# Retention attention and an MLP on one core: block 6's first product by seven half-size products, q and k turned each on its own landing, later scores, a new order

## The chip, the cores and the metric

The kernel runs on one core of a Trainium2 chip. The metric is device time in microseconds (us), the median of several runs. Beside the timed runs there is one profiled execution with a trace; its span is the time from the first to the last instruction that the profiler recorded.

## The reference

Eight batches of eight heads, 576 positions, 64 values per head. Position i attends to all j up to i with a weight that falls as gamma^(i-j), without softmax. The heads are joined to 512 values per token (4608 tokens), and a two-layer MLP with exact gelu follows.

```python
scores = scale * np.matmul(q, k.transpose(0, 1, 3, 2))
gamma = 1.0 - 2.0 ** (-5.0 - np.arange(H))
Dmat = np.where(rel >= 0, gamma ** rel, 0.0)      # rel = i - j
attn = np.matmul(scores * Dmat, v)
x = attn.transpose(0, 2, 1, 3).reshape(B * S, H * D)    # 4608 x 512
g = gelu(x @ w_in)                                       # 512 x 2048
out = g @ w_out                                          # 2048 x 512
```

## The kernel before, in words

**Units and blocks.** The attention is cut into 36 units, numbered 0 to 35: a unit is 128 positions of one batch (or the last 64 positions of two batches together). From unit 4 on, units are handled in groups of two batches (4 and 5, ..., 33 and 34), with the short ones alone (10, 17, 26, 35). Four units in a row make one block of 512 tokens for the MLP; there are nine blocks, 0 to 8. Unit n belongs to block n // 4.

**A group's way through the attention.** Its q, k and v are loaded and cast to bf16 by DMAs issued on POOL (`load`, L318). q and k are turned so that the head's 64 values lie on the partitions: for the first seven groups by TensorE (`turn`, L478), for all later ones by transposing DMAs issued on SP's queue (`turn_dma`, L489), which also carries most of the stores of the output (L718). Then follow the scores (`scores`, L526, for a short unit L516, into four or two PSUM banks), the mask on VectorE (`masked`, L549 and L545), the product with v (`inner`, L591 or L582), the running state of the recurrence (`state`, L610), the part of the earlier positions (`cross`, L642) and the copy of the result to the tile xT (`evacuate`, L661 or L457). v is scaled beforehand (`scaled_v`, on VectorE L566 or, for units in the set BY_ACT, in eight pieces on ACT, L563).

**The first product of a block** (x @ w_in) is made in the ordinary way for blocks 0 to 6 (`mlp1`, L690): 16 pieces of 128 rows of d_ff, each four matmuls of up to 512 columns, then the gelu on ACT (L699). From block FAST on (7 before) it is made by seven products of half size in place of eight (`fast`, L955, a Strassen scheme in Winograd's form). The products are named P1 to P7; d_ff is cut in four groups j of 512, a group has seven products of four matmuls of 256 columns. They need sums of blocks of w_in (`sum_in`, L913 to L915, and `sum_last`, L920, which overwrites a part of w_in once block FAST - 1 has read it) and sums of blocks of x (`sum_x`, L928). Between the products there are copies of a bank (P1 and P7, L452 on VectorE or L457 on ACT, whichever the planner thinks free), additions on VectorE (P6 L970, P5 L974), and the gelus (L976, L980).

**The second product** (g @ w_out) is made by `mlp2` (L735) for block 0 and in the same seven-product way for blocks 1 to 8 (`part`, L874, with sums of g on VectorE, L771 to L775, and `after` for what follows each product).

**What sets the order.** Every engine works through its own list of instructions in order. The lists are written by a planner that runs while the kernel is built: it keeps a reckoned clock for each engine (`T`), reckoned landings for DMAs (`hw_dma`, `sw_dma`), and a main loop (L1179 on) that appends, at each step, the work that is ready by this reckoning: X (cross), U (state), S (inner and/or scores), T (turn), or a piece of the MLP (`mlp_pick`). `fire` (L1121) lists what other engines do beside it: loads in the order of ORDER, sums, scaled v, and the transposing DMAs. The runs of the MLP are first product, second product, block after block; a second product and the seven-product first product of the next block are mixed piece by piece (kinds "3" and "4"), up to two groups j at a time.

**ORDER** (L330) lists the loads (`q5`, `wi3` a piece of w_in, `wo2` a piece of w_out, `io` constants, `dq3` a decay table), and among them numbers that steer the planner: `a8` puts unit 8's scaled v on ACT; `s20+3.0` lets the scores of the group that begins with unit 20 be listed only 3.0 us after the turn's reckoned landing; `b17+2.0` does the same for the product with v of unit 17. nA counts the units that are scored, nB those multiplied with v, nX those finished, nD the groups whose turn by DMA is listed.

Of the kernel before, what the change touches and what calls it, by code (L numbers as in the profile page):

```python
# [17 lines left out]
def kernel(  # L18
# [14 lines left out]
    nc = tc.nc  # L33
# [13 lines left out]
    NCI = -(-S // C)  # L47
# [4 lines left out]
    units = [(bp, 0, j) for bp in range(2) for j in range(2)]  # L52
# [7 lines left out]
    N_U = len(units)  # L60
# [7 lines left out]

    N_PE_TR = 7
    HW_FIRST = ((("q", 0),), (("k", 0),))  # L70
    FAST, ALL_FAST = 7, 7
    N_LD = 5
    N_QKT = 4
    N_VH = 6
# [250 lines left out]
    for x, keys in enumerate(zip(*HW_FIRST)):  # L325
        for n, (what, i) in enumerate(keys):
            land[what, i] = (4.6, 5.2)[n] + 0.75 * x
            t = tiles_of(i)
            cast_due[what, i] = (t[1] if what == "v" else t[0][:, "qk".index(what)], first[what, i])
    ORDER = ("wi1 q1 k1 wi0 io q2 k2 v0 v1 q3 wi2 v2 wi3 k3 wi4 v3 q4 wi5 wi6 q5 k4 a8 dq2 k5 wo1 wi7 wo0 v5 v4 "  # L330
# [4 lines left out]
             "b22+3.0 s23+2.0 s15+0.3 s13+3.0").split()  # L335

    BY_ACT = {int(x[1:]) for x in ORDER if x[0] == "a"}
    S_LATE = {int(x[1:].split("+")[0]): float(x.split("+")[1]) for x in ORDER if x[0] == "s"}
    B_LATE = {int(x[1:].split("+")[0]): float(x.split("+")[1]) for x in ORDER if x[0] == "b"}
    ORDER = [x for x in ORDER if x[0] not in "abs"]  # L340

    rest = const.tile([128, 2], BF16, name="rest")

# [137 lines left out]
        release(b, done + 0.05)  # L481
        sg[n]["T"] = max(sg[n].get("T", 0.0), done + SEM)

    def turn_dma(n):
        qk, qkT = loaded[groups[n][0]][0], qkT_of(n)
        short = units[groups[n][0]][2] is None
        rows = TAIL if short else C
        for jj in range(2):
            nc.sync.dma_start(qkT[:, jj, :, 0:rows], qk[0:rows, jj].rearrange("p h j d -> p (h j d)"), transpose=True)  # L489
            ends = sg[n].setdefault("ends", {})  # L490

            def put(end, jj=jj):
                ends[jj] = end
                sg[n]["T"] = max(ends.values()) + SEM

            hw_dma(1.3, MOVE["turn"] * (0.62 if short else 1.0), max(land["qk"[jj], i] for i in groups[n]), put)

    def scores(n):
        g = groups[n]
# [121 lines left out]

    def state_at(bp, ci):
        at = u_ready.get((bp, ci - 1), 1e9) if ci else 0.0
        return max([at] + [st[i].get("V", 1e9) if "Bdone" in st[i] else 1e9 for i in pair_of[bp, ci]])

    def reload():
# [372 lines left out]
    def fast_ready(t, j, p):  # L999
        if any((t, n) not in xs_at for n in range(4)) or any((2 * j + x, y) not in wi_at for x in range(2) for y in range(2)):  # L1000
            return 1e9
        at = max([xs_at[t, {P7: 1, P6: 2, P4: 3}.get(p, 0)]] + [wi_at[2 * j + x, y] for x in range(2) for y in range(2)])
        if p == P1:
            if not may_begin(t, j):
                return 1e9
            if wanted[0] and lead()[0] == "3" and lead()[2] in (M3, M4, M1) or len(held) + 3 + pending() > 7:
                return 1e9
            if t >= ALL_FAST and nA < N_U and lead()[0] == "3":
                return 1e9
            if j == 2 and t < ALL_FAST and (t - 1, M1, 0) not in begun:  # L1010
                return 1e9
            return max(at, free_time(2))
        if p == P7:
            return max(at, free_time(1), f_at.get(((t, j - 2), "V"), f_at.get(((t - 1, j + 2), "V"), 0.0) if j < 2 else 1e9))
        at = max(at, f_at[(t, j), {P6: P1, P2: P1, P5: P6, P4: P6, P3: P5}[p]])
        return max(at, free_time(1)) if p == P6 else at
# [104 lines left out]
    def fire():  # L1121
        nonlocal nD, nV
        now = T["pe"]
        while ORDER and T["pool"] <= now + 1.5 and next_order():
            pass
        while T["dve"] <= now + 1.5:
            one = min((x for x in queued if x[0] <= now + 0.2 and may_sum(*x[2:])), key=lambda x: x[1], default=None)
            if one is None:
                break
            queued.remove(one)  # L1130
            one[2](*one[3])
        if FAST < N_BLK and len(wi_sum) < 3 * (N_DF // 2) and first_block() >= 3 and T["dve"] <= now + (0.0 if first_block() < FAST - 1 else 0.8):
            sum_in(len(wi_sum) // 3)
        for mm in list(wi_read):
            if (mm, 0) in wi_at and T["dve"] <= now + 1.0 and wi_at[mm, 0] <= now + 0.3 and wi_read[mm] <= now + 0.3:
                sum_last(mm)
                del wi_read[mm]
        t = xs_next[0]
        if (t < N_BLK and all(4 * t + y in x_at for y in range(4)) and (t == FAST or all((t - 1, j) in f_done for j in range(0, N_DF // 4, 1 + (t - 1 < ALL_FAST))))
                and max(x_at[4 * t + y] for y in range(4)) <= now + 0.3 and T["dve"] <= now + 1.0):  # L1140
            sum_x(t)
            xs_next[0] += 1
        for key in [x for x in cast_due if land[x] <= now + 0.2]:
            dst, src = cast_due.pop(key)
            land[key] = either(0.7, land[key], dst, src) + SEM
        while later:
            n = next((n for n, x in enumerate(later) if x[0] <= now and T[x[1]] <= now + 0.25
                      and (x[1] == "dve" or x[0] < 5.0 or all(y[3] is not make_args for y in later))), None)
            if n is None:
                break  # L1150
            _, engine, dur, fn = later.pop(n)
            fn()
            on(engine, dur, now)
        while nV < N_U and nV < len(s_done) + N_VH and ("v", v_order[nV]) in land and ("v", v_order[nV]) not in cast_due:
            i = v_order[nV]
            if land["v", i] + 0.1 > now or nA <= i or i in kept and nA < 8 or i in raw and (T["act"] if i in BY_ACT else T["dve"]) > now + 2.0 * (nA > 8):
                break
            scaled_v(i)
            nV += 1
        while (nD < len(groups) and nD < group_of[min(nX, N_U - 1)] + N_QKT  # L1160
               and all((what, i) in land and land[what, i] - 0.3 <= now for what in "qk" for i in groups[nD])):
            turn_dma(nD)
            nD += 1
            store_kept()

    def warm(n):
# [12 lines left out]
    while True:  # L1179
# [21 lines left out]
        if nA < N_U:  # L1201
            n = group_of[nA]
            if n < nT or N_PE_TR <= n < nD:
                g, scored = groups[n], sg[n]["T"] + S_LATE.get(nA, 0.0)
        back = list(range(nB, nA))
        if nB < nA:
            if early:
                back = [nB]
            first_o = units[nB][1] == 0 and units[nB][2] == 0
            ready = max(max(st[i]["R"], land["v", i] if i in raw and nA < 8 else st[i].get("V", 1e9)) for i in back)  # L1210
            if any(("v", i) in cast_due for i in back):
                ready = 1e9
            ready = max(ready + B_LATE.get(back[0], 0.0), free_time(out_banks(back) + first_o))
            hurry = early or nA == N_U or stuck
            if not hurry and first:
                kind, t = first[0], first[1]
                hurry = nB < 4 * t + 4 if kind in "14" else len(runs[0]) <= (20 if t + 1 >= FAST else 6) and nB < 4 * t + 8
            if hurry:
                n = out_banks(back) + first_o + 2 * len(g)
                along = not early and nA >= 4 and scored <= now and len(frees(n)) == n and free_time(n) <= now + 0.3  # L1220
                cand(ready, "S", g if along else [], back)
        if g and scored < 1e8:
            if early or stuck:
                cand(max(scored, free_time(2 * len(g))) if nA - nB <= 2 else 1e9, "S", g, [])
            else:
# [4 lines left out]
                if (free and all(st[i]["R"] <= now and st[i].get("V", 1e9) <= now + 0.3 for i in back)  # L1230
                        and nA + len(g) <= ahead):
                    n = 2 * len(g) + out_banks(back) + any(units[i][1] == 0 for i in back)
                    wanted[0] = scored <= now and nA < 4 * (first[1] - (first[0] == "4")) + 12
                    if n + len(held) + pending() <= 8 and T["dve"] <= now + 1.0:
                        cand(max(scored, free_time(n) - 0.3), "S", g, back)
                    elif n > 7 and n - 2 * len(g) + len(held) + pending() <= 8:
                        cand(free_time(n - 2 * len(g)) - 0.3, "S", [], back)
# [52 lines left out]
        soon = [x for x in (land[key] for key in cast_due)] + [x[0] for x in queued] + [T["dve"] for x in queued]  # L1290
        if nV < N_U and ("v", v_order[nV]) in land and nV < len(s_done) + N_VH:
            soon += [land["v", v_order[nV]] + 0.1, T["dve"] - 1.9]
        if nD < len(groups) and all((x, i) in land for x in "qk" for i in groups[nD]):
            soon.append(max(land[x, i] for x in "qk" for i in groups[nD]) - 0.3)
        if wanted[0]:
            soon += [T["dve"] - 1.0 + 0.01]
        waits = [w for w in waits + soon if w > now and w < 1e8]
# [37 lines left out]
```

## Time and profile before

| | us |
|---|---|
| median of three timed runs | 287.1 (286.86 to 287.55) |
| profiled execution | 288.85 |
| its span | 287.1 |
| granted TensorE clock | 1.00 |

Costly groups of the page, busy us and instructions: first product L690 101.7 (624 matmuls), second product L874 46.8 + 32.2 + 30.6 (912), seven-product first product of blocks 7 and 8 L955 33.4 in four rows (224); on VectorE the masks L549 30.2 + 10.3, sums of g 21.7 + 21.4 + 13.3; on ACT the gelus L699 66.2. The DMA engines are busy nearly all the time until some 210 us, first with loads; POOL issues the last load at 179.8 us.

How to read it: PE is TensorE's matmuls, PEld its weight loads, DVE is VectorE, ACT ScalarE, POOL GpSimd, SP the queue of SyncE. A group's mean is that of an instruction from its start to its end; matmuls overlap, so the spacing of a stream is read from the chain (length divided by count). The chain of waits is the work that ended last, followed back.

### The profile page before, as it was taken

The numbers are of one execution on the slowest core, as the hardware profiler recorded it, in microseconds if no ns is written. First come the engines' busy times: TensorE is split into PE (matmuls) and PEld (weight loads), VectorE is DVE, ScalarE is ACT, GpSimd is POOL, SyncE is SP. The second block draws the span as 40 slices with busy tenths as digits, with TensorE's granted clock in tenths as the row PEclk, the third lists the DMA queues.
The fourth block names the chain that finished last, engine by engine and source line by source line (L and its number), as shares of the span: only waits on it lengthen the run. The fifth ranks groups of instructions, "written<-read, shape, count | busy, mean of one in ns | idle before, by whom it ended". The sixth has DMA issues, their size and how long they took to land.

```text
span 287.1 us, 7914 instructions
## 1 busy us (share of the span) xinstructions
PE 278.1 (97%) x3310; PEld 202.3 (70%) x3310; DVE 192.1 (67%) x400; ACT 153.2 (53%) x346; POOL 114.0 (40%) x143
## 2 busy tenths in 40 slices
PE   7989999999999999899999999999999999999994
PEld 2568677578864688348855686468755888888893
DVE  4834682789865795788098817673589659966922
ACT  4956436664549524773258438872566363565320
POOL 8997888995245355325667434100000000000000
PEclk9999999999999999999999999999999999999999
DMA  9999999999999999999999999990220000400234
GB/s 144 169 178 184 187 182 156 142 124 128 159 153 249 157 134 127 156 196 147 167 177 165 147 135 138 219 103 1 75 75 0 2 0 2 146 2 1 75 110 112
DMA packets 152803, 35.38 MB, mean 123 GB/s; under 512 B 141120, under 2 KB 148928, under 8 KB 152768
## 3 DMA queue, kind: packets, MB, share of 16 engines
q0 software_dynamic: 116832, 18.10, 93.7%
q1 hardware_dynamic: 34528, 16.26, 34.8%
q10 hardware_dynamic: 1408, 0.52, 0.7%
q8 instruction: 26, 0.43, 0.6%
q14 instruction: 9, 0.07, 0.1%
HBM read 36.70 MB, written 9.44 MB: 161 GB/s over the span
## 4 chain that ended last, share of the span: by engine, by line
PE 76%; DMA 16%; POOL 4%; DVE 2%; issue 1%; POOLq 0%; SPq 0%
PE m L874 28%; PE hT L690 26%; PE f L955 9%; DMA qk_ld<-in_q_dram 5%; PE oT L735 5%; DMA qk_ld<-in_k_dram 4%; DMA qkT<-qk_ld 4%; DMA qk<-in_k_dram 3%; PE o_ps L591 2%; PE sc L526 2%; POOL qk L318 2%; PE qk_ps L478 1%; POOL w_in L291 1%; PE u_ps L610 1%; PE o_ps L642 1%; POOL v_ld L318 1%
## 5 line engine op out<-in xcount | busy, mean ns | idle before, releaser
L690 PE MATMUL hT<-xT,w_in 128*128 128x512 bf16 (+3 forms) x624 | 101.7, 319 | 0.0
L699 ACT ACTIVATE g<-hT 128x512 bf16<-128x512 f32 (+2 forms) x121 | 66.2, 564 | 41.6 <-PE hT L690 41.1
L690 PEld LDWEIGHTS <-w_in 128*128 128x128 bf16 x624 | 54.7, 98 | 39.9
L874 PEld LDWEIGHTS <-gs 128*128 128x128 bf16 x656 | 62.3, 98 | 7.6
L874 PE MATMUL m<-w_sum,gs 128*128 128x256 bf16 (+1 forms) x400 | 46.8, 268 | 0.1
L318 POOL DMA_DIRECT2D v_ld<-in_v_dram x40 | 34.1, 860 | 22.3 <-DMA qk_ld<-in_k_dram 11.3
L549 DVE TENSOR_TENSOR ret<-sc,msk 128x512 bf16<-128x512 f32 x48 | 30.2, 682 | 15.2 <-PE sc L526 15.0
L318 POOL DMA_DIRECT2D qk_ld<-in_k_dram x36 | 30.3, 850 | 23.1 <-DMA qk_ld<-in_q_dram 21.0
L318 POOL DMA_DIRECT2D qk_ld<-in_q_dram x36 | 30.6, 855 | 19.2 <-DMA qkT<-qk_ld 5.4
L874 PE MATMUL m<-w_out,gs 128*128 128x256 bf16 x256 | 32.2, 273 | 0.0
L874 PE MATMUL m<-w_sum,g 128*128 128x256 bf16 x256 | 30.6, 273 | 0.0
L563 ACT ACTIVATE vh<-v_ld,dv 128x64 bf16<-128x64 bf16 x112 | 27.9, 337 | 0.0
L874 PEld LDWEIGHTS <-g 128*128 128x128 bf16 x256 | 25.1, 98 | 4.0
L771 DVE TENSOR_TENSOR gs<-g 128x1024 bf16<-128x1024 bf16 x32 | 21.7, 686 | 7.6 <-ACT g L699 7.4
L661 DVE TENSOR_TENSOR xT<-o_ps,dqT 128x512 bf16<-128x512 f32 (+1 forms) x32 | 18.4, 616 | 5.4 <-PE o_ps L642 5.1
L775 DVE TENSOR_TENSOR gs<-g 128x1024 bf16<-128x1024 bf16 x32 | 21.4, 682 | 0.0
L457 ACT COPY o<-m 128x512 f32<-128x512 f32 x14 | 8.2, 585 | 22.8 <-PE m L874 22.8
L826 DVE SCALAR_TENSOR_TENSOR o<-m,o 128x512 f32<-128x512 f32 (+1 forms) x9 | 5.6, 629 | 18.7 <-PE m L874 10.1
L980 ACT ACTIVATE g<-f 128x512 bf16<-128x512 f32 x24 | 13.6, 591 | 6.9 <-PE f L955 6.9
L457 ACT CAST u_sb<-u_ps 128x512 bf16<-128x512 f32 x14 | 8.2, 585 | 16.4 <-PE u_ps L610 16.4
L735 PE MATMUL oT<-w_out,g 128*128 128x512 bf16 x64 | 15.5, 380 | 0.0
L549 DVE TENSOR_TENSOR ret<-sc,near 128x512 bf16<-128x512 f32 x16 | 10.3, 683 | 7.2 <-PE sc L526 6.0
(96 smaller groups left out, 303.9 us busy)
## 6 DMA issues: line engine op xcount, KB each, us to landing
out_dram<-o SPq DMA_DIRECT2D x27, 256.0 KB, 7.1
v_ld<-in_v_dram POOLq DMA_DIRECT2D x32, 128.0 KB, 8.9
qk_ld<-in_q_dram POOLq DMA_DIRECT2D x28, 128.0 KB, 9.6
qk_ld<-in_k_dram POOLq DMA_DIRECT2D x28, 128.0 KB, 10.7
w_in<-in_moe_w_in_dram POOLq DMA_DIRECT2D x8, 256.0 KB, 6.8
w_out<-in_moe_w_out_dram POOLq DMA_DIRECT2D x8, 256.0 KB, 8.2
out_dram<-o SPq DMA_DIRECT2D x14, 128.0 KB, 2.3
qk_ld<-in_k_dram POOLq DMA_DIRECT2D x8, 64.0 KB, 9.6
```

The source lines that it names most:

```text
L318: nc.gpsimd.dma_start(dst, src[2 * bp + jj, :, ci * C:ci * C + n, :].rearrange("h s d -> s h d"))
L457: nc.scalar.copy(dst, src)
L549: nc.vector.tensor_tensor(r, t, by, op=ALU.mult)
L563: nc.scalar.activation(vh[:, h, :], loaded[i][1][:, h, :], AF.Copy, scale=dv[:, h, ci:ci + 1])
L661: nc.vector.tensor_tensor(x_of(i)[:, :, n * x:n * x + n], o, dqT[:, :, ci * C:ci * C + n], op=ALU.mult)
L690: nc.tensor.matmul(hT[:, m, :], lhsT=w[:, cc, o:o + 128], rhs=x_tiles[t][:, cc, lo:hi], start=(cc == 0), stop=(cc == N_DM - 1))
L699: nc.scalar.activation(g_of(t, m0 // 2)[:, m0 % 2:m0 % 2 + n, lo:hi], hT, AF.Gelu)
L735: nc.tensor.matmul(oT, lhsT=g_of(t, m // 2)[:, m % 2, cols], rhs=w_out_sb[m // 2][:, m % 2, :], start=(m == 0), stop=(m == N_DF - 1))
L771: nc.vector.tensor_tensor(s.rearrange("p m a b -> p m (a b)"), g[:, :, 0, :], g[:, :, 1, :], op=ALU.add)
L775: nc.vector.tensor_tensor(s, g[:, :, :, LEFT], g[:, :, :, RIGHT], op=MINUS)
L874: nc.tensor.matmul(m[:, 0 if apart else ts, :], lhsT=a, rhs=w[:, c0:c1], start=p in begins and mm == 0 and ts == 0, stop=mm == N_DF // 2 - ...
L955: nc.tensor.matmul(m[:, y, :], lhsT=a[:, c], rhs=d[:, c], start=p in (P1, P7) and y == 0 and c == 0, stop=c == 1, skip_group_check=True)
```

## The change

Seven edits, all in the code that the planner runs.

- FAST and ALL_FAST go from 7 to 6: block 6's first product is made by seven half-size products too, all four groups of it. The sums of w_in are then made once for blocks 6, 7 and 8, and those of x for block 6 as well.
- `turn_dma` lists the transposing DMA of q or of k alone, as soon as that one's loads are reckoned landed (`turnable`); before, both were listed when both had landed.
- Groups that are turned by DMA have their scores listed 2.5 us behind the turn's reckoned landing where ORDER has no number for them (before 0).
- The beginning of a seven-product group: the old rules (not while attention is left, and a rule on the third group) make room for a list, P_WAIT (`p25+35`: group 1 of block 6, number 4 x 6 + 1, not before 35 units are scored).
- Two more numbers per unit or block: DVE_LAG (`z`), how far VectorE's reckoned clock may be ahead when scores are listed (before 1.0 for all), and HURRY (`u`), when waiting units' products are listed ahead of the MLP's pieces.
- `state_at` keeps the second state of a pair of batches behind the last unit of the pair before.
- ORDER is another list.

```diff
@@ -68,7 +68,7 @@
 
     N_PE_TR = 7
     HW_FIRST = ((("q", 0),), (("k", 0),))
-    FAST, ALL_FAST = 7, 7
+    FAST, ALL_FAST = 6, 6
     N_LD = 5
     N_QKT = 4
     N_VH = 6
@@ -327,17 +327,21 @@
             land[what, i] = (4.6, 5.2)[n] + 0.75 * x
             t = tiles_of(i)
             cast_due[what, i] = (t[1] if what == "v" else t[0][:, "qk".index(what)], first[what, i])
-    ORDER = ("wi1 q1 k1 wi0 io q2 k2 v0 v1 q3 wi2 v2 wi3 k3 wi4 v3 q4 wi5 wi6 q5 k4 a8 dq2 k5 wo1 wi7 wo0 v5 v4 "
-             "wo3 wo2 q6 wo6 q8 dq3 wo7 v7 wo4 k6 k7 wo5 q7 v6 v9 v11 k9 q9 k8 k10 s4+0.6 q10 k11 k12 v8 q12 a29 "
-             "v10 dq4 s31+0.6 s27+6.0 a27 a6 a20 q11 v12 a28 a7 s34+4.0 a19 b6+0.3 b21+1.5 b7+2.0 s21+3.0 b10+4.0 "
-             "s8+0.6 s11+0.3 b17+2.0 s32+6.0 b19+6.0 s2+0.3 b23+1.0 b18+1.0 s18+1.0 a13 s16+0.3 a11 s20+3.0 "
-             "s29+6.0 s10+1.5 a14 a25 b2+0.6 b20+4.0 a32 s25+6.0 b15+0.3 b13+3.0 s12+0.6 a33 s14+0.3 s26+0.6 "
-             "b22+3.0 s23+2.0 s15+0.3 s13+3.0").split()
+    ORDER = ("wi1 k1 wi0 io q1 v0 q2 k2 v1 wi2 v2 k3 wi3 q3 v3 wi4 wi5 wi6 k4 q5 k5 q4 v5 wi7 wo1 wo0 k6 v4 dq2 "
+             "wo2 wo3 q7 wo4 k7 dq3 q11 b4+1.0 wo6 v8 wo5 q6 k8 wo7 v6 v7 k9 q10 q9 a28 k11 q8 v11 k10 q12 dq4 v9 "
+             "v10 a5 k12 v12 b19+6.0 a24 a27 a26 s4+1.5 z32+3 z8+5 b11+1.5 a23 z23+2.2 s2+0.6 p32+28 p31+28 z18+5 "
+             "z31+1.6 s21+1.0 s14+1.5 b14+4.0 z19+0.6 z5+0.3 z13+5 s10+4.0 z27+2.2 z34+2.2 b17+1.0 a0 b3+1.0 "
+             "p25+35 z30+0.3 p33+26 z28+0.3 z17+2.2 s1+1.0 s31+6.0 z16+0.3 z4+0.3 z22+0.6 s16+3.0 s23+3.0 b22+0.3 "
+             "a14 b16+2.0 b15+2.0 a11 z14+3 p35+31 s27+0.6 z10+5 z20+2.2 s9+4.0 a18 a30 z12+2.2 s22+3.0 s35+0.6 "
+             "s8+1.5 s29+0.6 z15+5 u2+8 b5+0.3 p28+29 s5+6.0 s26+1.5 p26+28 b13+2.0 p29+29 u5+20 s19+4.0 p24+31 a7 "
+             "a20 b9+1.0 s24+0.3 s28+0.6 a17 b18+3.0 a22 u4+28 b12+1.5 s33+1.5 s7+1.5 s30+0.3 u8+0 s32+4.0 z21+0.6 "
+             "b21+6.0").split()
 
     BY_ACT = {int(x[1:]) for x in ORDER if x[0] == "a"}
     S_LATE = {int(x[1:].split("+")[0]): float(x.split("+")[1]) for x in ORDER if x[0] == "s"}
     B_LATE = {int(x[1:].split("+")[0]): float(x.split("+")[1]) for x in ORDER if x[0] == "b"}
-    ORDER = [x for x in ORDER if x[0] not in "abs"]
+    DVE_LAG, P_WAIT, HURRY = ({int(x[1:].split("+")[0]): float(x.split("+")[1]) for x in ORDER if x[0] == kind} for kind in "zpu")
+    ORDER = [x for x in ORDER if x[0] not in "abszpu"]
 
     rest = const.tile([128, 2], BF16, name="rest")
 
@@ -481,19 +485,24 @@
         release(b, done + 0.05)
         sg[n]["T"] = max(sg[n].get("T", 0.0), done + SEM)
 
-    def turn_dma(n):
+    def turn_dma(n, jj):
         qk, qkT = loaded[groups[n][0]][0], qkT_of(n)
         short = units[groups[n][0]][2] is None
         rows = TAIL if short else C
-        for jj in range(2):
-            nc.sync.dma_start(qkT[:, jj, :, 0:rows], qk[0:rows, jj].rearrange("p h j d -> p (h j d)"), transpose=True)
-            ends = sg[n].setdefault("ends", {})
-
-            def put(end, jj=jj):
-                ends[jj] = end
-                sg[n]["T"] = max(ends.values()) + SEM
-
-            hw_dma(1.3, MOVE["turn"] * (0.62 if short else 1.0), max(land["qk"[jj], i] for i in groups[n]), put)
+        nc.sync.dma_start(qkT[:, jj, :, 0:rows], qk[0:rows, jj].rearrange("p h j d -> p (h j d)"), transpose=True)
+        ends = sg[n].setdefault("ends", {})
+
+        def put(end):
+            ends[jj] = end
+            sg[n]["T"] = max(ends.values()) + SEM
+
+        hw_dma(1.3, MOVE["turn"] * (0.62 if short else 1.0), max(land["qk"[jj], i] for i in groups[n]), put)
+
+    def turnable(now):
+        if nD >= len(groups) or nD >= group_of[min(nX, N_U - 1)] + N_QKT:
+            return None
+        return next((jj for jj in range(2) if jj not in sg[nD].get("ends", {})
+                     and all(("qk"[jj], i) in land and land["qk"[jj], i] - 0.3 <= now for i in groups[nD])), None)
 
     def scores(n):
         g = groups[n]
@@ -621,6 +630,8 @@
 
     def state_at(bp, ci):
         at = u_ready.get((bp, ci - 1), 1e9) if ci else 0.0
+        if bp and ci == 1 and nX <= units.index((bp - 1, NCI - 1, None)):
+            return 1e9
         return max([at] + [st[i].get("V", 1e9) if "Bdone" in st[i] else 1e9 for i in pair_of[bp, ci]])
 
     def reload():
@@ -1005,9 +1016,7 @@
                 return 1e9
             if wanted[0] and lead()[0] == "3" and lead()[2] in (M3, M4, M1) or len(held) + 3 + pending() > 7:
                 return 1e9
-            if t >= ALL_FAST and nA < N_U and lead()[0] == "3":
-                return 1e9
-            if j == 2 and t < ALL_FAST and (t - 1, M1, 0) not in begun:
+            if nA < P_WAIT.get(4 * t + j, 0):
                 return 1e9
             return max(at, free_time(2))
         if p == P7:
@@ -1157,10 +1166,12 @@
                 break
             scaled_v(i)
             nV += 1
-        while (nD < len(groups) and nD < group_of[min(nX, N_U - 1)] + N_QKT
-               and all((what, i) in land and land[what, i] - 0.3 <= now for what in "qk" for i in groups[nD])):
-            turn_dma(nD)
-            nD += 1
+        while True:
+            jj = turnable(now)
+            if jj is None:
+                break
+            turn_dma(nD, jj)
+            nD += len(sg[nD]["ends"]) == 2
             store_kept()
 
     def warm(n):
@@ -1201,7 +1212,7 @@
         if nA < N_U:
             n = group_of[nA]
             if n < nT or N_PE_TR <= n < nD:
-                g, scored = groups[n], sg[n]["T"] + S_LATE.get(nA, 0.0)
+                g, scored = groups[n], sg[n]["T"] + S_LATE.get(nA, 2.5 if n >= N_PE_TR else 0.0)
         back = list(range(nB, nA))
         if nB < nA:
             if early:
@@ -1214,7 +1225,7 @@
             hurry = early or nA == N_U or stuck
             if not hurry and first:
                 kind, t = first[0], first[1]
-                hurry = nB < 4 * t + 4 if kind in "14" else len(runs[0]) <= (20 if t + 1 >= FAST else 6) and nB < 4 * t + 8
+                hurry = nB < 4 * t + 4 if kind in "14" else len(runs[0]) <= HURRY.get(t, 8 if t + 1 >= FAST else 16) and nB < 4 * t + 8 + 4 * (t + 1 >= FAST)
             if hurry:
                 n = out_banks(back) + first_o + 2 * len(g)
                 along = not early and nA >= 4 and scored <= now and len(frees(n)) == n and free_time(n) <= now + 0.3
@@ -1231,7 +1242,7 @@
                         and nA + len(g) <= ahead):
                     n = 2 * len(g) + out_banks(back) + any(units[i][1] == 0 for i in back)
                     wanted[0] = scored <= now and nA < 4 * (first[1] - (first[0] == "4")) + 12
-                    if n + len(held) + pending() <= 8 and T["dve"] <= now + 1.0:
+                    if n + len(held) + pending() <= 8 and T["dve"] <= now + DVE_LAG.get(nA, 1.0):
                         cand(max(scored, free_time(n) - 0.3), "S", g, back)
                     elif n > 7 and n - 2 * len(g) + len(held) + pending() <= 8:
                         cand(free_time(n - 2 * len(g)) - 0.3, "S", [], back)
@@ -1290,8 +1301,10 @@
         soon = [x for x in (land[key] for key in cast_due)] + [x[0] for x in queued] + [T["dve"] for x in queued]
         if nV < N_U and ("v", v_order[nV]) in land and nV < len(s_done) + N_VH:
             soon += [land["v", v_order[nV]] + 0.1, T["dve"] - 1.9]
-        if nD < len(groups) and all((x, i) in land for x in "qk" for i in groups[nD]):
-            soon.append(max(land[x, i] for x in "qk" for i in groups[nD]) - 0.3)
+        if nD < len(groups):
+            for x in "qk":
+                if all((x, i) in land for i in groups[nD]):
+                    soon.append(max(land[x, i] for i in groups[nD]) - 0.3)
         if wanted[0]:
             soon += [T["dve"] - 1.0 + 0.01]
         waits = [w for w in waits + soon if w > now and w < 1e8]
```

## The prediction

> **What bounds the kernel now.** I read the busy table first, then PE's waits, then the chain of waits in order of time, then the busy time by stretch. In the first line the reader is to see that TensorE (PE) is busy nearly all the time; the next three are all that PE waited for after its first instruction (waited-for time, times, longest).
>
> ```profile
> PE 278.1 (97%) x3310; PEld 202.3 (70%) x3310; DVE 192.1 (67%) x400; ACT 153.2 (53%) x346; POOL 114.0 (40%) x143
> ```
>
> ```profile
> PE sc L526 <- DMA qkT<-qk_ld: 1.7, 1, 1.7
> PE qk_ps L478 <- DMA qk<-in_k_dram: 1.2, 1, 1.2
> ...
> PE qk_ps L478 <- DVE qk L452: 0.5, 1, 0.5
> ```
>
> So of 287.1 us, PE is idle for 9.0: 1.2 before it starts, the 3.4 of these waits, 0.3 of smaller gaps, and 4.1 at the end, where the last output is stored. The first 19.4 us also hold 30 warm-up matmuls (9.4 us), so work begins to be plentiful there. After that a us of matmuls taken away is a us off the span, unless something new makes PE wait. The chain of waits around block 6 (start, length, what) shows this without a hole, and gives the price of the two kinds of product:
>
> ```profile
> 205.95 6.91 PE hT L690 x32
> 212.85 0.57 PE o_ps L591 x16
> 213.42 0.25 PE u_ps L610 x16
> 213.67 0.30 PE sc L516 x12
> ...
> 214.27 3.56 PE hT L690 x16
> 217.83 0.25 PE o_ps L582 x16
> 218.07 0.13 PE o_ps L642 x16
> 218.20 3.56 PE hT L690 x16
> 221.76 2.18 PE m L874 x20
> 223.94 0.87 PE f L955 x8
> ```
>
> The hT lines are block 6's first product, 64 matmuls of 512 columns; f at L955 is block 7's, already made by seven half-size products. Between them lie the last attention units: unit 35's scores start at 213.67.
>
> **Part 1, block 6's first product.** 6.91 / 32 = 0.216 us for a matmul of 512 columns, 0.873 / 8 = 0.109 for one of 256. Removed: 64 x 0.216 = 13.82 us. Added: four groups of d_ff, seven products each, four matmuls in a product: 112 x 0.1092 = 12.23. PE saves 1.59 us. Nothing hides this: PE is the engine whose end sets the end here, and blocks 7 and 8 show (no PE wait from 221.8 to 283) that such products interleaved with a second product can run without a hole.
>
> The page TensorE: Matmul & The Clock Gate of the Trainium skill (Back-to-back issue gap) speaks against this: in a stream with weight loads it has about 131 ns for a matmul of 512 columns and 81 for one of 128. By a line between these two (an estimate from that page, some 98 ns at 256) the removed work would be 8.4 us, the added 10.9, and the change would cost 2.5. Its other formula there, columns / 2.4 + 2.5 ns, gives 215.8 and 109.2 and so the saving above. This trace has 216 and 109, and decides for the second.
>
> **What this adds on other engines.** By the rows of blocks 7 and 8: 8 additions on VectorE (L970, L974; 0.69 us each, 5.5 us), 8 copies from PSUM (P1, P7) that go to ACT or VectorE, whichever is free (0.58 or 0.69 each), and one set of sums of x (L928, 1.5). The gelus stay 16 in number. Were half the copies VectorE's, it gets 5.5 + 2.8 + 1.5 = 9.8 us more. The sums of w_in (L913 to L915) are not added but shared with blocks 7 and 8, and are made at 113 to 140 us already; their last part (L920, 8 x 0.28) moves from block 6's stretch to the end of block 5's. The busy time by stretch (length, then PE, PEld, DVE, ACT, POOL) says whether there is room:
>
> ```profile
> 178.00:192.00 14.00, 14.00 (x146) 7.02 (x139) 10.13 (x18) 12.43 (x33) 1.35 (x2) 1.00 1.59 179
> 192.00:206.00 14.00, 14.00 (x195) 12.31 (x192) 6.22 (x12) 4.72 (x12) 0.00 (x0) 1.00 0.11 38
> 206.00:222.00 16.00, 16.00 (x164) 7.97 (x163) 15.19 (x35) 10.45 (x20) 0.00 (x0) 1.00 0.10 35
> 222.00:244.00 22.00, 22.00 (x204) 19.70 (x203) 15.60 (x26) 10.47 (x19) 0.00 (x0) 1.00 0.01 1
> ```
>
> VectorE has 47.1 us of 66 here; with 9.8 more in 64.4 it is at 88%, with all copies on ACT at 84%; ACT goes from 38.1 to at most 43. So the sum fits, if the work is spread: 206 to 222 is nearly full (15.2 of 16), 192 to 206 is not half full, and block 6's products now begin there, beside block 5's second product. The cover of Part 1 is thin: for two groups at a time, PE has 6.1 us of work (56 x 0.109), and one group's own chain P1, copy, P6, addition, P5, addition, P3 is about 4 x 0.44 for products, 4 x 0.25 for the tail of each matmul (0.60 busy for 4, of which 0.44 spacing: 0.16; I take 0.25 with the signal) and 3 x 0.69, 4.8 us. I cost it at nothing. Ends: 0 and 3.4, if every one of 12 such steps meets a VectorE pair of masks ahead of it (1.29 for the pair, L549, less about 1 of other work each would be 0.28).
>
> Extra matmuls that only mark a bank (L407) don't occur before; one costs as L735's, 0.216. None to two; I take none.
>
> **Part 2, the turns.** The words say that q and k are turned by DMAs issued together; the diff lists the one whose data is reckoned to have landed, without waiting for the other. No DMA is added: 30 transposes, 1.2 to 5.2 us of SP's queue each (median 2.3), 9.9 us to landing. What moves is q's, past stores of SP's queue; a transpose listed early holds the stores behind it until its load lands, and nobody waits for a store soon. The one PE stall (1.7 us at 120.6, units 20 and 21) shows how little this gives: the chain before it is q's load, k's load (12.86 us), then k's transpose (110.81 to 122.26, 11.45 us). The k load came last, and q's turn had been issued already. Gain taken: nothing; ends -1.7 (this stall) and +1.7 (another such).
>
> **Part 3, the scores' margin.** Scores of units from 10 on are listed 2.5 us behind the reckoned landing, where no number stands in the list. Units 11, 15, 17, 18 go from 0.3, 0.3, 0, 1.0 to 2.5, 22 from 0 to 3.0, 33 from 0 to 1.5; units 20 and 21, those that stalled, go from 3.0 to 2.5, and 27 and 29 from 6.0 to 0.6. Matmuls of the MLP fill the delay at no cost. Ends again -1.7 and +1.7; since more margins grow than shrink, but not that of the one that stalled, I take a quarter of the stall, -0.4. This is a choice, not a measurement.
>
> **Part 4, the new order.** Loads ahead of the first block: k1 before q1, v0 four places earlier, q3 and k3 complete at the same place as before (twelve loads ahead, 0.7 to 0.95 us of POOL each). The 1.2 us wait at 18.2 to 19.4 is for unit 3's k; it may go, or a like one may come: ends -1.2 and +1.2, taken 0. The hand-set places of the small work (which vh go to ACT, how late a unit's second product is listed) move work on engines with room; 0.
>
> **Sum.** -1.59 - 0.4 = -2.0. The profiled execution took 288.85, its span of 287.10 and 1.75 around it; it would be 286.85, with a span of 285.1. The three timed runs have a median of 287.1, 1.75 under the profiled one, so the 1.7 us stall may be absent from them; this is why only a quarter of it is counted. Taken off their median: **285.1 us**.
>
> **The rivals.**
>
> *VectorE or the PSUM banks eat the saving* (no change, 286.5 to 287.7). For it: 88% load on an engine that works in order, and 15.2 of 16 us at 206 to 222. Against: 71% was carried in 222 to 244 with no hole, ACT is free to take the copies, and block 6's sums of g (7.1 us) may fall later than before. At the 12 steps, 0.13 us each is enough to lose 1.59.
>
> *The gate* (slower). The new list lets group 1 of block 6 begin only when 35 units are scored, that is unit 35 alone left, and group 0 when 31 are; during the second product of block 5 the banks are taken, and in this trace units 33 and 34 are scored at 204.17, near its end, and unit 35 at 213.67. The scores of 33 and 34 open the gate; where they stand now they do no harm. But if the order or the DMAs bring units 33 and 34 to where unit 35 was, PE has block 6's group 0 (28 x 0.109 = 3.06 us) to put in place of the 6.91 us of hT that stood at 205.95 to 212.85, and waits 3.85: +3.85 - 1.59 = +2.3, 289.4 us. It decides from a start of those scores later than 205.95 + 3.06 = 209.0; at 210.6 the saving is gone. Against: the last transposes are issued by 189.1 and land within 9.7 us, so by 199.
>
> *More stalls go* (283.9 to 282.6): the saving with the whole stall of 1.7 is -3.3, 283.8; with the early 1.2 too, 282.6. For it: wider margins; against: units 20 and 21.
>
> *Weight loads pace the small matmuls.* Each matmul of 256 columns needs a load of 98 ns; were these not hidden, 112 x (98 + 109) = 23.2 us would stand against 13.8, +9.4, 296.5 us. L955's spacing of 109 with such loads speaks against it. The rule of the Trainium skill quoted in Part 1 leans this way too, by less; the trace disagrees with it (216 ns at 512 columns).
>
> **How the numbers follow.** Forecast 0.56 (284.3 to 286.3), more stalls gone 0.15, no change 0.13, the gate 0.15, weight loads 0.01. Within 0.2% (0.57 us, about what a measurement of this kernel can tell from no change) is 286.5 to 287.7. Faster: 0.56 + 0.15 + 0.01 (the edge of the third case) = 0.72; same 0.12; slower 0.16. The range 283.9 to 287.5 holds the forecast, two thirds of the better case and nearly all of no change, 0.56 + 0.10 + 0.13 = 0.79, and the bounds of the stall terms but for both at their ends.
>
> **What would show it.** Part 1: 64 matmuls of 512 columns fewer at L690, 336 instead of 224 at L955, and no PE wait from 190 us on; PE's busy time down by some 1.6. Gate: a PE hole before an f line right after scores (L526, L516). VectorE: PE waits at L955 for L970, L974 or copies, VectorE busy above 90% there. Parts 2 and 3: whether PE sc L526 still waits for qkT. Wrong altogether if PE's busy time falls and its idle time grows by more.

## The result, and the profile after

The changed kernel takes 285.48 us (median of six, 285.29 to 286.5), the kernel before, timed beside it, 287.0; the ratio is 0.9949, 95% interval 0.9932 to 0.9965. In a later series it took 285.62 (twelve runs), 0.9939 (0.9917 to 0.9961). The profiled execution took 285.49, its span 283.7, so 1.79 lie around it.

The busy table of the changed kernel, and all that PE waited for (us in total, times, longest):

```profile
PE 278.0 (98%) x3361; PEld 207.6 (73%) x3361; DVE 199.7 (70%) x412; ACT 158.8 (56%) x362; POOL 114.0 (40%) x143
```

```profile
PE warm L1187 <- DVE zeros L118: 1.2, 1, 1.2
PE hT L701 <- DMA w_in<-in_moe_w_in_dram: 0.8, 1, 0.8
```

There are 51 matmuls more (48 for block 6, three more to warm up) and 7.6 us more VectorE. This execution has no wait of the scores for qkT, and no wait at all after 19 us. PE's busy time hardly fell (278.1 to 278.0): against the 1.6 us less in block 6 stand 1.0 more in the first 19.4 us, three more warm-up matmuls among it (17.4 us busy for 16.4); the rest is small. The chain of waits at block 6 of the changed kernel (start, length, what):

```profile
189.57 0.57 PE o_ps L600 x16
190.39 0.57 PE sc L535 x32
191.18 0.97 PE hT L701 x4
192.15 2.18 PE m L885 x20
194.34 0.87 PE f L966 x8
195.21 0.87 PE m L885 x8
196.08 0.87 PE f L966 x8
...
217.91 0.57 PE o_ps L600 x16
218.73 0.35 PE o_ps L653 x16
219.08 2.29 PE m L885 x20
221.37 0.87 PE f L966 x8
222.24 0.37 PE sc L525 x16
```

Block 6's products (f, L966) now begin at 194.3, two us into block 5's second product (m, L885), and alternate with it. Units 33 and 34 are scored ahead of that, at 190.4 (204.2 before); their product with v waits until 217.9, and unit 35's scores until 222.2. The busy time by stretch (length, then PE, PEld, DVE, ACT, POOL; last the granted clock and the DMA engines) shows what that does for VectorE:

```profile
192.00:206.00 14.00, 14.00 (x130) 12.55 (x129) 11.15 (x20) 7.10 (x13) 0.00 (x0) 1.00 0.01 1
206.00:222.00 16.00, 16.00 (x186) 14.12 (x183) 12.98 (x24) 8.21 (x16) 0.00 (x0) 1.00 0.18 68
222.00:244.00 22.00, 22.00 (x244) 19.38 (x242) 17.77 (x33) 12.23 (x23) 0.00 (x0) 1.00 0.04 10
```

From 6.2 of 14, 15.2 of 16 and 15.6 of 22 it has become 11.2, 13.0 and 17.8: a level load of some 81%, and PE is busy all through these 52 us.

### The profile page after: what moved, and what is told of

It is laid out like the page before. It is cut to its first block, busy times and chain, and to the rows that moved or that the text cites. A ratio compares the mean times of both kernels' runs of the same rounds, so it can differ in the third digit from the quotient of the medians.

```text
span 283.7 us, 8075 instructions
## 1 busy us (share of the span) xinstructions
PE 278.0 (98%) x3361; PEld 207.6 (73%) x3361; DVE 199.7 (70%) x412; ACT 158.8 (56%) x362; POOL 114.0 (40%) x143
## 4 chain that ended last, share of the span: by engine, by line
PE 92%; POOL 3%; DMA 3%; issue 0%; DVE 0%; POOLq 0%
PE m L885 35%; PE hT L701 29%; PE f L966 13%; PE oT L746 5%; PE o_ps L600 3%; PE sc L535 3%; DMA w_in<-in_moe_w_in_dram 3%; POOL qk L318 2%; PE o_ps L653 1%; PE u_ps L619 1%; PE qk_ps L482 1%; POOL v_ld L318 1%; POOL w_in L291 1%; PE sc L525 0%; PE o_ps L591 0%
## 5 line engine op out<-in xcount | busy, mean ns | idle before, releaser
L701 PE MATMUL hT<-xT,w_in 128*128 128x512 bf16 (+3 forms) x560 | 87.4, 312 | 0.8 <-DMA w_in<-in_moe_w_in_dram 0.8
L710 ACT ACTIVATE g<-hT 128x512 bf16<-128x512 f32 (+2 forms) x106 | 57.7, 556 | 36.9 <-PE hT L701 36.1
L701 PEld LDWEIGHTS <-w_in 128*128 128x128 bf16 x560 | 48.4, 98 | 33.8 <-DMA w_in<-in_moe_w_in_dram 1.0
L885 PEld LDWEIGHTS <-gs 128*128 128x128 bf16 x656 | 62.2, 98 | 7.7
L885 PE MATMUL m<-w_sum,gs 128*128 128x256 bf16 (+1 forms) x400 | 47.7, 268 | 0.0
L885 PE MATMUL m<-w_out,gs 128*128 128x256 bf16 x256 | 32.5, 273 | 0.0
L885 PE MATMUL m<-w_sum,g 128*128 128x256 bf16 x256 | 30.9, 273 | 0.0
L572 ACT ACTIVATE vh<-v_ld,dv 128x64 bf16<-128x64 bf16 x120 | 30.0, 339 | 0.0
L885 PEld LDWEIGHTS <-g 128*128 128x128 bf16 x256 | 24.9, 98 | 3.9
L991 ACT ACTIVATE g<-f 128x512 bf16<-128x512 f32 x36 | 20.2, 590 | 8.9 <-PE f L966 7.5
L966 PEld LDWEIGHTS <-w_in 128*128 128x128 bf16 x192 | 18.8, 98 | 2.2
L987 ACT ACTIVATE g<-p 128x512 bf16<-128x512 f32 x12 | 7.6, 630 | 14.1 <-DVE p L985 14.1
L966 PEld LDWEIGHTS <-wi 128*128 128x128 bf16 x144 | 14.0, 98 | 1.6
```

Of the source, the lines that this page charges most:

```text
L572: nc.scalar.activation(vh[:, h, :], loaded[i][1][:, h, :], AF.Copy, scale=dv[:, h, ci:ci + 1])
L701: nc.tensor.matmul(hT[:, m, :], lhsT=w[:, cc, o:o + 128], rhs=x_tiles[t][:, cc, lo:hi], start=(cc == 0), stop=(cc == N_DM - 1))
L710: nc.scalar.activation(g_of(t, m0 // 2)[:, m0 % 2:m0 % 2 + n, lo:hi], hT, AF.Gelu)
L885: nc.tensor.matmul(m[:, 0 if apart else ts, :], lhsT=a, rhs=w[:, c0:c1], start=p in begins and mm == 0 and ts == 0, stop=mm == N_DF // 2 - ...
L966: nc.tensor.matmul(m[:, y, :], lhsT=a[:, c], rhs=d[:, c], start=p in (P1, P7) and y == 0 and c == 0, stop=c == 1, skip_group_check=True)
L991: nc.scalar.activation(g[:, :, rows, cols], m, AF.Gelu)
```

## The experiments

Times are medians; the ratio is to the kernel before, timed in the same series. My theory: PE sets the end, so block 6's matmuls are the gain. Rivals: the order, the turns or the margins bring it; or VectorE sets the pace there.

**The kernel before again.** No edit.

> The kernel before, unchanged, profiled a second time. My theory (block 6's matmuls are the whole gain, and the 1.7 us stall at units 20 and 21 was there in the first profile alone): a span near 285.3 us and no wait of the scores for qkT above 0.5 us. The rival (the stall is there in most executions, and the later scores removed it): a wait of 1 to 2 us again, with a span near 287.

287.28 us against 286.89, ratio 1.0023 (1.0008 to 1.0037), although nothing differs: its twelve runs lie between 286.69 and 288.94, while half of the 29 beside it lie between 286.76 and 287.02. So 0.2% between two kernels of one series is not to be read. Its profiled execution (span 285.0) has no wait for qkT:

```profile
PE warm L1176 <- DVE zeros L118: 1.2, 1, 1.2
PE qk_ps L478 <- DMA qk<-in_q_dram: 0.6, 1, 0.6
PE oT L735 <- issue: 0.3, 2, 0.2
```

(The last row is no wait: two matmul records are missing there.) So the 1.7 us stall is not in every execution of the kernel before. It isn't the first profile's alone either: the run with the margin alone, further down, has it again at the same scores.

**The new order with block 6's first product in the ordinary way.**

```diff
-    FAST, ALL_FAST = 6, 6
+    FAST, ALL_FAST = 7, 7
```

> The changed kernel with block 6's first product made in the ordinary way again: all of the order, margins and turns of the change, without its matmuls. My theory: 287.0 us, ratio 1.000 (between 0.998 and 1.003). The rival that order, margins and turns bring the gain: 285.5 us, ratio 0.995. A ratio above 1.005 would say that the new order fits only with the half-size products.

287.43 us, 1.0018 (0.9999 to 1.0037). As my theory had it; the order, the turns and the margins bring nothing without the half-size products. POOL's and SP's lists are those of the changed kernel, PE's, but for one piece of four matmuls, up to 192 us, block 5's second product. From the start of that product to the last matmul its trace takes 89.4 us, the changed kernel's 88.0: this 1.4 us is block 6 alone.

**Sixteen more matmuls in block 6.**

```diff
+        if t == 6 and p == P1:
+            for y in range(2):
+                for c in range(2):
+                    nc.tensor.matmul(m[:, y, :], lhsT=w_in_sb[2 * j + y][:, c, 0:128], rhs=x[:, c, LEFT],
+                                     start=y == 0 and c == 0, stop=c == 1, skip_group_check=True)
         done = pe(4 * 0.1092, 4)
```

> The changed kernel with P1 of block 6 made twice (the second time over the first, same result): 16 more matmuls of 256 columns, 1.75 us of PE's work, which the planner does not know of. My theory (PE has no slack in block 6): 285.5 + 1.75 = 287.2 us, ratio to before 1.001. The rival (VectorE or ACT sets the pace of block 6, PE has slack): under 286.0 us, ratio 0.997 or less.

287.16 us, 1.0018 (1.0005 to 1.0031), 1.5 to 1.7 us above the changed kernel's medians (2.0 by the ratios) for 1.75 us of matmuls; in the traces, from the start of block 5's second product to the last matmul, 1.74. The other engines' lists are unchanged. PE has no slack in block 6: what is added there, or taken away, is paid or gained.

**The old order with block 6 in half-size products.**

```diff
-    FAST, ALL_FAST = 7, 7
+    FAST, ALL_FAST = 6, 6
```

> The kernel before with block 6's first product by half-size products and nothing else of the change. My theory (PE sets the end; the matmuls alone are worth 1.59 us): 0.9945 of before if the old rules spread the work well enough, 285.4 us. Rival one (the old rules hold block 6's products back until the last scores, and VectorE has no room): holes of PE in front of f lines, 1.6 us or more in sum, ratio 1.000 or above. Rival two (the gain is the new order's): ratio 1.000 with no holes.

291.18 us, 1.0147 (1.0130 to 1.0165): 4.3 us slower than before, with the same PE list as before until block 5's second product is done. So the matmuls saved are not enough; 5.9 us are lost elsewhere. By the trace, block 5's second product and all behind it take 95.2 us for 91.1 in the second profile of the kernel before; with the 1.6 us saved that is 5.6 lost there, nearly all in holes between 204 and 230 us. PE's longest waits there, and its stretches:

```profile
PE o_ps L582 <- DVE vh L566: 1.2, 1, 1.2
...
PE f L955 <- DVE f L970: 0.8, 3, 0.3
PE f L955 <- DVE p L974: 0.4, 1, 0.4
PE f L955 <- ACT f L457: 0.4, 1, 0.4
```

```profile
192.00:206.00 14.00, 13.71 (x190) 11.88 (x188) 6.52 (x14) 5.75 (x15) 0.00 (x0) 1.00 0.11 39
206.00:222.00 16.00, 14.13 (x173) 11.52 (x171) 14.38 (x25) 8.31 (x16) 0.00 (x0) 1.00 0.09 34
222.00:244.00 22.00, 20.52 (x215) 17.96 (x215) 16.53 (x31) 11.01 (x21) 0.00 (x0) 1.00 0.01 1
```

VectorE is busy for less than half of block 5's second product (6.5 of 14 us), as before. Then block 6's products, without another product beside them, and the masks and copies of units 33 to 35 all stand in VectorE's list at once, and PE, which takes its list in order, is idle for 1.9 us and then 1.5. Its first f matmul starts at 203.84, after the second product, where the changed kernel's starts at 194.17.

**The old order, with group 0 of block 6 let in earlier** (on top of the edit above).

```diff
-            if t >= ALL_FAST and nA < N_U and lead()[0] == "3":
-                return 1e9
-            if j == 2 and t < ALL_FAST and (t - 1, M1, 0) not in begun:
+            if t == 6 and nA < {24: 31, 25: 35, 26: 36, 27: 36}.get(4 * t + j, 0):
+                return 1e9
+            if t > 6 and nA < N_U and lead()[0] == "3":
                 return 1e9
```

> The kernel before with block 6 in half-size products, as in the run of the old order, but group 0 of block 6 may begin beside block 5's second product once 31 units are scored; groups 1 to 3 wait until all 36 are. My theory (what matters is a partner for the products and room on VectorE where the last units stand): between the two, ratio 1.004 to 1.012, holes at f lines of 1.5 to 3 us. The rival that the beginning does not matter: 1.0147 as without it. The rival that it is all: 0.996 or less.

291.31 us, 1.0135 (1.0106 to 1.0165): no better, against my expectation. Group 0 begins at 192.2, but the waits come back for the other three groups, at the same two places:

```profile
PE f L955 <- DVE f L970: 2.3, 2, 1.2
...
PE f L955 <- DVE p L974: 1.2, 2, 0.8
PE o_ps L642 <- DVE u_sb L452: 0.6, 1, 0.6
PE f L955 <- DVE xT L661: 0.5, 1, 0.5
```

```profile
206.00:222.00 16.00, 12.93 (x200) 10.32 (x189) 15.59 (x27) 8.16 (x20) 0.00 (x0) 1.00 0.14 53
```

VectorE at 15.6 of 16 us, PE idle for 3.1. So a partner for a quarter of the products doesn't help while the last units' attention work stands where it stood.

**The new order with the old rules for the beginning.**

```diff
-            if nA < P_WAIT.get(4 * t + j, 0):
+            if t >= ALL_FAST and nA < N_U and lead()[0] == "3":
+                return 1e9
+            if j == 2 and t < ALL_FAST and (t - 1, M1, 0) not in begun:
                 return 1e9
```

> The changed kernel with the two old rules for the beginning of a group of half-size products in place of the list P_WAIT: no group of block 6 begins beside block 5's second product while a unit is unscored. In the changed kernel unit 35 is scored at 222, so block 6's 12.2 us of products lose their partner. My theory (the interleaving is what keeps PE full): block 6's first f line comes after block 5's second product, with holes of 2 to 4 us in sum, ratio to before 1.000 to 1.010. The rival (VectorE's total work is the cause of the old order's holes, not when the products begin): no new holes, ratio 0.995.

286.46 us, 0.9973 (0.9953 to 0.9992): about half of the gain is kept, and in the best runs (285.50) nearly all. My theory had missed that the planner would move the last units: under the old rules it scores units 33 and 34 at 192.5 and unit 35 at 200.3, in the middle of block 5's second product, so block 6 begins at 201.5 and still has half of it as a partner. Its profiled execution lost 2 us ahead of that, 1.3 of it by waits for qkT, in a stretch whose PE list is the changed kernel's. The rules are those of the old order's run, but its holes are not there (one f line waits, 0.2 us): what differs is the rest of the new order, which puts the last units elsewhere. Which of its many entries it takes for that was not separated. The list P_WAIT by itself does nothing: with it emptied every engine's list is the same, instruction by instruction.

**Scores without the margin.**

```diff
-                g, scored = groups[n], sg[n]["T"] + S_LATE.get(nA, 2.5 if n >= N_PE_TR else 0.0)
+                g, scored = groups[n], sg[n]["T"] + S_LATE.get(nA, 0.0)
```

> The changed kernel with scores listed at the turn's reckoned landing where the list has no number (0 for 2.5 us; units 11, 13, 15, 17, 18, 20 among others). My theory: PE waits for qkT once or twice, 0 to 2 us in some executions, ratio to before 0.995 to 1.000. The rival that the margin does nothing: 0.9949 as the whole change has it. The rival that the margin costs (scores later than they could be): below 0.993.

288.46 us, 1.0051 (1.0029 to 1.0074), worse than I expected: 2.9 us above the changed kernel by ratio, between 286.47 and 290.94 but for one. The profiled execution is the fastest of them, and even it waits for qkT, 0.9 us (its two longest waits):

```profile
PE warm L1187 <- DVE zeros L118: 1.2, 1, 1.2
PE sc L535 <- DMA qkT<-qk_ld: 0.9, 1, 0.9
```

The slower executions have no trace, so that they lose their 2 us and more in the same waits is likely but not shown.

**The margin alone, on the kernel before.**

```diff
-                g, scored = groups[n], sg[n]["T"] + S_LATE.get(nA, 0.0)
+                g, scored = groups[n], sg[n]["T"] + S_LATE.get(nA, 2.5 if n >= N_PE_TR else 0.0)
```

> The kernel before with the margin alone: scores 2.5 us behind the reckoned landing where its list has no number (units 17, 22, 24, 33, 35). My theory (the executions of before differ by 0 to 2 us in waits for qkT, and the margin takes some of it): ratio 0.998 to 1.000, less spread. The rival that the margin is worth nothing by itself: 1.000 to 1.001 with the same spread. A gain of 0.995 or more would make it the cause of the whole change.

287.19 us, 1.0001 (0.9977 to 1.0026), spread as before (286.61 to 289.41). But the edit hardly changed the kernel: four matmuls of PE change places at 103 us, and every other engine's list is the same. So this is nearly the kernel before again, and says little of what a margin is worth; units 20 and 21 have a number of their own (3.0) and keep it. Its profiled execution (289.41) stalls where the first profile did, at the scores of units 20 and 21:

```profile
PE sc L526 <- DMA qkT<-qk_ld: 1.4, 1, 1.4
```

That the new order needs its margins is what the run before this one shows.

**q and k turned together.**

```diff
-            turn_dma(nD, jj)
-            nD += len(sg[nD]["ends"]) == 2
+            turn_dma(nD, 0)
+            turn_dma(nD, 1)
+            nD += 1
```

(`turnable` then waits for both landings.)

> The changed kernel with q's and k's turn listed together once both have landed, as before the change. My theory (k's load comes last, so q's turn alone opens nothing): ratio 0.995, up to 0.998 as the planner's order moves with it. The rival (each turn on its own landing is needed): PE waits for qkT of 2 us or more in sum, ratio above 1.000.

287.39 us, 1.0009 (0.9994 to 1.0023): 1.7 us worse than the changed kernel by ratio; its profile has no wait for qkT, but a moved order. Its profile has 1.0 us of PE waiting for a sum of g, and block 5's second product begins 1.4 us later. In the changed kernel a transpose has 1.56 us of SP's queue and 8.7 to landing (medians), before 2.33 and 9.9. The size is measured; by which path the order moved is not settled.

**VectorE doubled in block 6, then in block 7.** P6's addition made twice.

```diff
-            nc.vector.tensor_tensor(to[1], f_bank[key, "p7"], m, op=ALU.add)
+            for _ in range(2 if t == 6 else 1):
+                nc.vector.tensor_tensor(to[1], f_bank[key, "p7"], m, op=ALU.add)
```

> The changed kernel with P6's addition on VectorE made twice in block 6 (the second time the same result): four more instructions of 0.69 us in the middle of the four chains, 2.8 us, which the planner does not know of. My theory (VectorE has the room, PE the work beside it): 0 to 0.6 us, ratio to before 0.995 to 0.997. The rival (VectorE is at its limit in block 6): 2 us or more, ratio above 1.001.

286.90 us, 1.0007 (0.9994 to 1.0020). PE's list is the same, the first f line comes at the same time (194.1), PE's last matmul ends at 281.4 for 280.0: 1.4 us for 2.8. Neither theory's number. To see whether the attention in block 6 makes it so, the same for block 7 (`t == 7`):

> The changed kernel with P6's addition on VectorE made twice in block 7, not in block 6. Doubled in block 6 it cost about half of its 2.8 us. My theory now (in block 6 the last attention units share VectorE with the products; block 7 has them behind it, but for units 35's): 0.3 us or less, ratio 0.995 to 0.997. The rival (any addition on such a chain costs, since the next product waits for it): again some 1.4 us, ratio 1.000.

287.01 us, 0.9994 (0.9972 to 1.0015), 1.4 us above the changed kernel timed beside it: my second guess fell. PE's waits, first with block 6 doubled, then block 7:

```profile
PE f L966 <- DVE f L982: 0.6, 2, 0.3
```

```profile
PE f L966 <- DVE f L982: 1.1, 2, 0.6
```

On average an added 0.69 us costs 0.35, in block 7 as in block 6, but the steps are uneven. By the starts of the same matmuls with and without the second addition, PE falls back by 0.22, 0.11, 0.44 and 0.17 us right behind the four in block 6 (the rest of the 1.4 comes later), and in block 7 by 0.71 and 0.60 behind the first and the last, and by 0.2 or less behind the others. So the cover that Part 1 of the prediction called thin runs from nothing to over half a us; the 1.3 us that its chain of 4.8 in 6.1 leaves for two groups is more than any of these places had.

**The changed kernel again.** No edit.

> The changed kernel, unchanged, beside the other kernels of this call. My theory (nothing but PE's work and rare DMA waits): ratio 0.995 again, between 0.993 and 0.997. The rival (its first runs were lucky): 0.998 or more, with waits of the scores for qkT.

285.62 us, 0.9939 (0.9917 to 0.9961), with one wait of 0.2 us after the start, none for qkT.

## Why the prediction was right, and where it was not

The time (285.48 for 285.1) and the first step, -1.59, were right. The other term, -0.4, isn't shown, and that the other engines cost nothing held only in the new order.

- **Part 1, -1.59.** The prices held: 0.87 for eight half-size matmuls in nearly every f line of the chain, 0.86 for four of 512 columns (2.59 for twelve). By the starts of the matmuls in the two traces, f gained 12.4 us and hT lost 13.8 beside its holes. The undone block 6 and the added matmuls both say that PE pays and gains here one for one. From the start of block 5's second product to the last matmul, the undisturbed execution of the kernel before takes 91.1 us (189.6 to 280.7), the changed one 88.0; of these 3.1, 1.61 are one attention group more that it has behind it by then (189.57 to 191.18), and 1.47 the saving.
- **The rule of 131 ns at 512 columns** (the Trainium skill, TensorE: Matmul & The Clock Gate, Back-to-back issue gap) would, by the estimate in Part 1, have made the change cost 2.5 us; the run with ordinary products in the new order is 1.8 us slower, not faster. The Trainium skill's other formula in that section (215.8 ns at 512 columns, 109.2 at 256) is the one that this trace agrees with, by its 216 and 109.
- **Other engines at nothing.** True of the kernel as changed, but only with its order, which the prediction priced at nothing (Part 4). The old order pays 5.9 us, so the rival "VectorE or the banks eat the saving" is real, and my 286.5 to 287.7 for it was too mild: 291.2. The step that was mis-sized is the bound of 3.4 us; it counted masks in front of single additions, not a whole stretch in which products, masks and copies queue in one list (15.6 of 16 us) with no other matmuls to run.
- **Part 2, nothing for the turns.** In the old order the k load came last, as said. In the new one, listing both together costs 1.7 us, through another order.
- **Part 3, -0.4.** The step as put, a quarter of a stall saved by wider margins, isn't shown; that the sum came out near the time is in this part luck. The stall is a matter of the execution: of five traces whose PE lists are those of the kernel before up to 190 us (but for the four matmuls named), two have it (1.7 and 1.4 us); of seven with the changed kernel's (but for one piece), one has it (1.1 us), at the same units. That is too few to call it rarer. The timed runs differ in spread: those of the kernel before lie, but for a few, up to 2 us above its fastest, those of the changed one mostly within 0.5. Median against median the gain is 1.5 to 1.8 us, fastest against fastest 1.6 (six runs each) and 1.1. But the run with ordinary products, with the changed kernel's PE list up to 190 us but for that piece, spreads over 2.3 us too. So what narrows the spread stays open.
- **Part 4, nothing for the order.** (v0 stands two places earlier in the new list, not four.) Between the second profile of the kernel before and the changed kernel's, 0.34 us is lost by the start of block 4's second product and 0.47 from there to block 5's. The second loss has no waits in it: the changed order breaks off the products of the MLP five times there in place of three to do attention work, and by the starts of the matmuls PE pays some 0.09 us at each entry (0.20 from a half-size matmul to the next, for 0.11) and 0.13 at each return; that makes some 0.3 of the 0.47. With these 0.81 off the 1.47, the last matmul ends 0.66 us earlier (280.01 for 280.67). The spans differ by 1.3, since from there to the end it is 4.3 us before and 3.7 after; why is not settled.
- **The gate** didn't decide: the list has no effect on the order. Scoring unit 35 at 222 did no harm, since groups 1 to 3 were already let in by units 33 and 34 at 190.4, as the prediction's bound (209.0) asks.

## What to carry to other kernels

Where one engine has no slack, work taken off it is worth its length, but only if the work that the trade adds elsewhere finds a place: read the neighbours' busy time in the stretch itself, and ask which independent work of the bounding engine will stand beside each new chain. The same edit cost 4.3 us in the old order and gained 1.5 to 1.8 in one that brought two attention units forward and spread the last ones. Where loads come by DMA, compare many executions: a stall in one trace need not be in the next of the same kernel, nor is it gone because the next has none.

## What the runs showed of the hardware

The same kernel, given twice to one chip, came out as 287.28 and 286.89 us, with the middle half of the runs over 1.3 and 0.3 us; and of its two traces one has PE waiting 1.7 us for a transposing DMA in its middle and the other not at all, with the same lists on every engine. So which DMA waits are met depends on more than the lists.

An addition of 0.69 us on VectorE in the middle of a chain of products costs 0.35 on average, from less than 0.1 to 0.7 by its place, with VectorE at some 81% in both blocks and PE otherwise never idle.

A change from one kind of matmul to another costs PE time without showing as a wait: 0.09 us from a half-size product to attention work, 0.13 on the way back.
